# Two buffers for the softmax sums, hops of the sums and of x set later than their producers, and w_in split at its first use

## The chip, the cores and the metric

The kernel runs on one core of one Trainium2 chip. The metric is the device time of one execution in microseconds; each time is a median of several runs of the same program. The core has five engines with queues of their own: TensorE (PE in the profile, its weight loads PEld), VectorE (DVE), ScalarE (ACT), GpSimd (POOL) and SyncE (SP), which here issues the DMAs of all loads and stores but the gathers and scatters of the last stage. Each queue is worked off in its order; an instruction at the head that waits holds what stands behind it.

## The reference

```python
q_n, k_n = rmsnorm(q, g_q), rmsnorm(k, g_k)              # 4 batches, 12 heads, 448 rows, 64 columns
attn = softmax(q_n @ k_n.T / sqrt(64))                   # sums + 1e-9 as the divisor
x = (attn @ v) with the heads side by side               # 1792 x 768
h = x @ w_in                                             # 768 x 2048, w_in in 64-bit floats
x = (h * clip(h + 3, 0, 6) / 6) @ w_out                  # 2048 x 768, w_out in 64-bit floats
logits = x @ w_gate                                      # 8 experts, each takes 224 rows, greedily
out[rows of e] = relu(x[rows of e] @ w1[e]) @ w2[e]
```

## The kernel before

All products run on float32 data split in a high and a low part (`xh`, `xl`; `wh`, `wl`), three matmuls for each product of two split operands. The attention is done in 24 head pairs, six to a batch. The first MLP product of a batch (16 units of 128 columns of `w_in`, 18 matmuls each) is cut in atoms and laid between the attention of the next batch's pairs; the last batch's follows the attention, and then come the second product, the routing and the experts, which the change does not touch.

The order of the attention stage is written by hand. `at(t, fn, ...)` enters an event at place t of a list; pair i begins at t = 16 i, and the constants `T_...` (L70 to L81) are places relative to that. The list is sorted, and every engine's queue gets its instructions in that order; `fill` hands out MLP atoms evenly in between, so that batch b's units lie between the places `ENDS[b]` and `ENDS[b+1]` (117 and 217 for batch 0, 313 for batch 1, 405 for batch 2). An event may stand ahead of another one's last use of the same buffer: it then waits.

For the pairs 6 to 22 the sums of the softmax make a way through memory: `padd` (GpSimd, L423) adds the exponentials `ph`, `psums` (L435) sums them on TensorE with a matrix of ones and copies the result with ScalarE into `rb` (L441, place 15.7), `rs_out` stores it (L445), `rs_in` loads it back in another layout (L450), `rec` takes reciprocals on DVE (L454), `r_out` stores them (L458), `r_in` loads them, broadcast, into the same `rb` (L464), `xmul` multiplies on GpSimd (L468), and `xsplit` makes `xh` on ScalarE (L478) and `xl` on GpSimd (L476). `rb` has one buffer. The pairs 0 to 5 and 23 take another way (L384 to L415) with no hops.

`w_in` and `w_out` arrive as 64-bit floats. `conv` (L148) narrows a unit: a load `wraw`, a copy on ScalarE (L139) and three operations on DVE (L140 to L142) into `cv` (two buffers), and a store to `w32` or `wo32` (L181, L179). For `w_in` it also makes the split: the high part on ScalarE (L171), the low part on GpSimd (L174), both in `whl` (one buffer), stored as `w_hl` (L176). The units of `w_in` lie at the places 20 + 10 u, those of `w_out` at 180 + 12 u. The first MLP products of the batches 0 to 2 then load a unit whole from `w_hl` (`win_whole`, L196, at atom `WD2` of the unit two before). For batch 3 `win_load` reads `w32` into a staging buffer and `win_split` (L191) makes both parts: high on ScalarE (L116), low on DVE for odd units and on GpSimd for even ones (L117). The tile `w` has three buffers. `g_out` stores a unit's result at atom `GD` of the next one.

Of the kernel before, what the change touches and what calls it, by code (L numbers as in the profile page):

```python
# [8 lines left out]
F32 = mybir.dt.float32  # L9
F32R = mybir.dt.float32r  # L10
BF16 = mybir.dt.bfloat16
I32 = mybir.dt.int32
AF = mybir.ActivationFunctionType
OP = mybir.AluOpType
# [7 lines left out]
def kernel(  # L22
# [14 lines left out]
    nc = tc.nc  # L37
    B, H, S, D = q.shape
# [5 lines left out]
    CP = 112  # L44
    NCH = S // CP
    NP = H // 2
    NC = DM // 128
    NF = FF // 128
    NTC = NT // 128
    NSL = NT // CP  # L50
    VB, CB = 4, 2
    WB = 6
    OB = 3
    PB = 12
# [12 lines left out]
    GR_, GG = 3, 2  # L67
    CI, CI0, CI1, CI2, CO = 6, 1.75, 2.5, 0.5, 1.5

    T_LOAD, T_VLOAD, T_NORM, T_Q, T_K, T_V = -72, -8, -38, -30, -28, 6  # L70
    T_SUMS, T_INV = -50, -42
    T_S1, T_MT = (-24, -23.9, -16, -15.9), -9
    T_ST = (0, 0.1, 8, 8.1)
    T_AV = ((17, 18, 19.5, 20.5), (22, 23, 24.5, 25.5))
    T_NUM, T_XT, T_MLP = 28, 33, (37, 41, 41, 37)
    T_ADD, T_PV, T_SUM = (6, 13), (15.6, 15.62, 15.64, 15.66), 15.7
    T_RS, T_RL, T_REC, T_RO, T_RB, T_X, T_XH, T_XL = 18, 21, 24, 25.5, 29, 35, 36, 38
    GD, WD2 = 6, 8
    C_ST, C_WH, C_WL, C_HL = 6, 7, 10, 13
    QMAJOR = tuple(range(NP)) + (B * NP - 1,)  # L80
    T_CI, D_CI, T_CO, D_CO, T_CL = 20, 10, 180, 12, 14  # L81

# [6 lines left out]
    dram = ctx.enter_context(tc.tile_pool(name="dram", bufs=1, space=DRAM))  # L89
# [34 lines left out]
    rawp = raw_stack.enter_context(tc.tile_pool(name="rawp", bufs=1, side="right"))  # L124
# [7 lines left out]
    wide = w_in.dtype == mybir.dt.int64  # L132
# [9 lines left out]
                lambda: nc.vector.scalar_tensor_tensor(vi, hi, -2147483648, vi, op0=OP.bitwise_and, op1=OP.bitwise_or))  # L142

    RAW = {}
    wide_b = range(B - 1) if wide else ()
    w_hl = [dram.tile([128, 2, 768], F32, name=f"w_hl{u}") for u in range(NF if wide else 0)]

    def conv(key, part):  # L148

        out_, n = key  # L150
        rows = slice(n * 128, (n + 1) * 128)
        if part < 0:
            raw = rawp.tile([128, 768, 2], I32, name="wraw", bufs=2)
            if out_:
                nc.sync.dma_start(raw.rearrange("p f t -> p (f t)"), w_out.bitcast(I32)[rows, :])
            else:
                nc.sync.dma_start(raw.rearrange("p (c f) t -> p c (f t)", c=NC),
                                  w_in.bitcast(I32)[:, n * 256:(n + 1) * 256].rearrange("(c p) f -> p c f", p=128))
            RAW[key] = raw
            return  # L160
        if part == 0:
            raw = RAW[key]
            v32 = rawp.tile([128, 768], F32, name="cv", bufs=CB)
            RAW[key] = (v32, narrow(raw[:, :, 0], raw[:, :, 1], v32))
        v32, steps = RAW[key][:2]
        if part < 4:
            steps[part]()
        elif part == C_WH:
            hl = rawp.tile([128, 2, 768], F32R, name="whl", bufs=1)
            RAW[key] += (hl,)  # L170
            nc.scalar.activation(hl[:, 0], v32, AF.Copy)  # L171
        elif part == C_WL:
            hl = RAW[key][2]
            nc.gpsimd.tensor_tensor(hl[:, 1], v32, hl[:, 0].bitcast(F32), op=OP.subtract)  # L174
        elif part == C_HL:
            nc.sync.dma_start(w_hl[n], RAW[key][2].bitcast(F32))  # L176
        elif part == C_ST:
            if out_:
                nc.sync.dma_start(wo32[rows, :], v32)  # L179
            else:  # L180
                nc.sync.dma_start(w32[:, rows].rearrange("(c p) f -> p c f", p=128), v32.rearrange("p (c f) -> p c f", c=NC))  # L181
# [4 lines left out]
    def win_load(u):  # L186
        v32 = stage("win_v").rearrange("p (c f) -> p c f", c=NC)
        nc.sync.dma_start(v32, src_in[:, u * 128:(u + 1) * 128].rearrange("(c p) f -> p c f", p=128))
        return u, v32

    def win_split(u, v32):  # L191
        w = wpool.tile([128, 2, NC, 128], F32R, name="w", bufs=WB // 2)
        split(v32, w[:, 0], w[:, 1], nc.vector if u % 2 else nc.gpsimd)
        return w[:, 0], w[:, 1]

    def win_whole(u):  # L196
        w = wpool.tile([128, 2, NC, 128], F32R, name="w", bufs=WB // 2)
        nc.sync.dma_start(w.rearrange("p a c f -> p a (c f)").bitcast(F32), w_hl[u])
        return w[:, 0], w[:, 1]


    a_stack = ExitStack()
    apool = a_stack.enter_context(tc.tile_pool(name="apool", bufs=2, side="left"))
# [32 lines left out]

    def vload(i):
        b, j = divmod(i, NP)
        t = apool.tile([CP, 2, NCH, D], F32, name="ld_v", bufs=1)
        nc.sync.dma_start(t.rearrange("p h c d -> p h (c d)"),  # L240
                          v[b, 2 * j:2 * j + 2].rearrange("h (p c) d -> p h (c d)", p=CP))
        QKV[i].append(t)
# [175 lines left out]
    PA, PV, RC, RB = {}, {}, {}, {}  # L418
# [16 lines left out]
    def psums(i):  # L435
        p = ps.tile([128, 512], F32, name="sm", tag="b", bufs=8)
        for n in range(2):
            for s, r in enumerate(ROWS):
                nc.tensor.matmul(p[r, :S], ones64, PA.pop((i, s, n)), start=(n == 0), stop=(n == 1))
        RB[i] = apool.tile([128, S], F32, name="rb", bufs=1)  # L440
        nc.scalar.activation(RB[i], p[:, :S], AF.Identity, bias=eps)  # L441

    def rs_out(i):
# [37 lines left out]

    late, tpool, ready, loaded = [], [], [], []
    units_in = list(range(NF)) * B
    whole = [len(wide_b) * NF]
    GB = 2

    def prefetch(splits=2):

        while whole[0] and len(ready) < splits:
            ready.append(win_whole(units_in.pop(0)))  # L490
            whole[0] -= 1
        if whole[0]:
            return
        while len(ready) < splits and loaded:
            ready.append(win_split(*loaded.pop(0)))
        while units_in and len(loaded) < 3 and (len(units_in) > NF or len(loaded) + len(ready) < 3 or tpool):
            loaded.append(win_load(units_in.pop(0)))

    def mlp1_atoms(b, inline):

        atoms = []
        state = {}

        def unit_start(f):
            if not ready:
                prefetch(1)
            if not ready:
                prefetch(1)
            state["w"] = ready.pop(0)
            if not whole[0]:  # L510
                prefetch()
            state["ps"] = ps.tile([128, 512], F32, name="h", tag="b", bufs=8)

        def mm(f, n):
            if n == 0:
                unit_start(f)
            c, t = divmod(n, 3)
            wh, wl = state["w"]
            xh, xl = XT[b]
            w = (wh, wh, wl)[t]  # L520
            x = (xh, xl, xh)[t]
            p = state["ps"]
            nc.tensor.matmul(p[:, :S], w[:, c], x[:, c], start=(n == 0), stop=(n == 3 * NC - 1))  # L523
            if n == 3 * NC - 1:
                r = mpool.tile([128, S], F32, name="r", bufs=1)
                nc.scalar.activation(r, p[:, :S], AF.Relu, bias=half, scale=1.0 / 6.0)
                g = mpool.tile([128, S], F32, name="g", bufs=GB)
                nc.vector.scalar_tensor_tensor(g, r, 1.0, p[:, :S], op0=OP.min, op1=OP.mult)
                state["g", f] = g
                if inline:  # L530
                    gsplit(b, f, g, nc.vector)

        def g_out(f):
            nc.sync.dma_start(g_dr[b][f * 128:(f + 1) * 128, :], state.pop(("g", f)))

        for f in range(NF):
            for n in range(3 * NC):
                atoms.append(lambda f=f, n=n: mm(f, n))
                if n == GD and f > 0:
                    atoms.append(lambda f=f: g_out(f - 1))  # L540
                if n == WD2 and b in wide_b:
                    atoms.append(prefetch)
                if inline and n == 10 and f > 1:
                    atoms.append(lambda f=f: lg(b, f - 2))
        atoms.append(lambda: g_out(NF - 1))
        if inline:
            for f in (NF - 2, NF - 1):
                late.append(lambda f=f: lg(b, f))
            late.append(lambda: lg_end(b, 0))
            late.append(lambda: lg_end(b, 1))  # L550
        return atoms
# [183 lines left out]
    for i in range(NH // 2):  # L735
        t = 16 * i
# [35 lines left out]
    for u in range(NF if wide else 0):  # L772
        for out_, t in ((0, T_CI + D_CI * u), (1, T_CO + D_CO * u)):
            at(t - T_CL, conv, (out_, u), -1)
            for part in (0, 1, 2, 3, C_ST) + (() if out_ else (C_WH, C_WL, C_HL)):
                at(t + part, conv, (out_, u), part)
    events.sort(key=lambda e: e[:2])
    ENDS = [8 * H * (b + 1) - 16 + T_MLP[b] for b in range(B)]
# [1 line left out]
    for t, _, fn, args in events:  # L780
        while now <= t:
            b = min(sum(now > e for e in ENDS), B - 1)
            end = ENDS[b]
            left = end - now
            w = 1
            if b == B - 1:
                z = end - max(now, 8 * NH + 4)
                left += (WT - 1) * z
                w = WT if now >= 8 * NH + 4 else 1
# [260 lines left out]
    for t in range(NTC):  # L1050
        a, z = t * 128, t * 128 + 128
# [130 lines left out]
    for pi, (t, hfs) in enumerate(passes):  # L1182
# [10 lines left out]
        for f in range(NF):  # L1193
            i, k = divmod(f, QF)
# [7 lines left out]
            wh, wl = wo[f]  # L1202
# [131 lines left out]
```

## Time and profile before

| | us |
|---|---|
| median of 3 runs | 1263.83 (1259.71 to 1263.83) |
| profiled execution, its own time | 1260.03 |
| its span, first to last instruction | 1258.2 |
| TensorE busy | 1161.1 (92%) |
| DVE busy | 779.1 (62%) |
| ScalarE busy | 549.4 (44%) |
| GpSimd busy | 505.8 (40%) |
| mean granted TensorE clock | 0.964 of full speed |

One execution was profiled. A matmul's end is modelled, so a busy TensorE need not be at its peak. Up to about 138 us of the span batch 0's attention runs alone, from there to about 565 us attention and MLP units are interleaved, to about 690 us the last batch's MLP runs, and then the rest. The granted clock has two levels, 1.2 and 2.4 GHz; a stretch's number is the mean of 0.5 and 1.

### The profile page before, as it was taken

Reading aid. Unit: us, or ns where it says so; the run is one execution under the profiler, and the core shown is the slowest. Engines: PE = TensorE matmul, PEld = TensorE weight load, DVE = VectorE, ACT = ScalarE, POOL = GpSimd, SP = SyncE. Lnnn points to the kernel's source line nnn. Section 1 sums busy time; section 2 is a strip of 40 time slices with the busy share of each in tenths; the row PEclk is TensorE's granted clock in tenths of the full one; section 3 lists DMA queues with packets and bytes.
Section 4 is the critical chain, followed back from the end, with each engine's and each line's share of the span. In section 5 each row is a group of like instructions: output and inputs, shape, how many; then the busy total and the mean of one; then the engine's idle time right before and its main releaser. Section 6 shows DMA issues by size and latency. Waiting matters only on the chain.

```text
span 1258.2 us, 19791 instructions
## 1 busy us (share of the span) xinstructions
PE 1161.1 (92%) x7204; PEld 943.5 (75%) x7204; DVE 779.1 (62%) x1572; ACT 549.4 (44%) x1019; POOL 505.8 (40%) x370
## 2 busy tenths in 40 slices
PE   4979998888999889999988999999999799999997
PEld 2777665665666667687766777777777799999997
DVE  7977866566567566424886466666667574555550
ACT  3645644543444445444664311111112575556650
POOL 2323654453344343211344222222224477766641
PEclk9977999899999999999998999999999899999999
DMA  3556898756655776656987422222224788877731
GB/s 106 176 192 205 277 317 258 265 195 209 239 208 193 242 238 242 237 181 197 304 261 236 129 76 61 71 63 76 64 76 118 213 249 257 244 236 236 223 123 44
DMA packets 200469, 237.14 MB, mean 188 GB/s; under 512 B 24338, under 2 KB 171444, under 8 KB 200372
## 3 DMA queue, kind: packets, MB, share of 16 engines
q1 hardware_dynamic: 197044, 224.88, 56.8%
q0 software_dynamic: 3328, 11.01, 2.8%
q8 instruction: 56, 0.92, 0.3%
q14 instruction: 41, 0.34, 0.1%
HBM read 184.87 MB, written 50.98 MB: 187 GB/s over the span
## 4 chain that ended last, share of the span: by engine, by line
PE 45%; DVE 7%; issue 5%; DMA 4%; ACT 2%; POOL 1%; POOLq 0%; SPq 0%; DVEq 0%; ACTq 0%
PE y L1138 15%; PE y L1286 8%; PE h L523 6%; PE h L1222 5%; PE h L1224 2%; DMA wo_s<-wo 2%; DMA we_s<-in_moe_w_dram 2%; PE rt L948 2%; DVE C L943 1%; DVE gl L561 1%; PE st L341 1%; PE av L430 1%; PE h L662 1%; PE xp L1170 1%; DVE wel L117 1%
## 5 line engine op out<-in xcount | busy, mean ns | idle before, releaser
L523 PE MATMUL h<-xh,w 128*128 128x448 f32 x768 | 245.2, 389 | 4.2 <-DVE mr L330 4.1
L523 PEld LDWEIGHTS h<-xh,w 128*128 128x128 f32 x768 | 147.4, 197 | 35.3 <-issue 16.1
L1081 POOL TENSOR_TENSOR g2l<-gr,g2h 128x512 fp32r<-128x512 f32 x60 | 79.1, 1320 | 206.7 <-ACT g2h L1079 159.5
L322 DVE TENSOR_REDUCE mx<-s 112x1 f32<-112x448 f32 x192 | 106.9, 613 | 70.0 <-PE s L319 69.9
L523 PE MATMUL h<-xl,w 128*128 128x448 f32 x384 | 147.0, 383 | 0.0
L1138 PE MATMUL y<-woh,g2l 128*128 128x512 f32 (+1 forms) x448 | 128.8, 349 | 1.0 <-POOL g2l L1081 1.0
L1079 ACT ACTIVATE g2h<-gr 128x512 fp32r<-128x512 f32 x60 | 37.9, 631 | 206.2 <-PE y L1138 158.5
L1138 PE MATMUL y<-woh,g2h 128*128 128x512 f32 (+1 forms) x448 | 127.7, 348 | 0.0
L1138 PE MATMUL y<-wol,g2h 128*128 128x512 f32 (+1 forms) x448 | 126.4, 346 | 0.0
L117 DVE TENSOR_TENSOR wel<-we_s,weh 128x768 fp32r<-128x768 f32 x59 | 78.7, 1341 | 60.6 <-ACT weh L116 60.6
L117 POOL TENSOR_TENSOR wel<-we_s,weh 128x768 fp32r<-128x768 f32 x48 | 97.1, 2028 | 44.5 <-ACT weh L116 37.9
L116 ACT ACTIVATE weh<-we_s 128x768 fp32r<-128x768 f32 x107 | 88.3, 841 | 60.1 <-DMA we_s<-in_moe_w_dram 41.8
L352 ACT ACTIVATE ph<-st 112x448 f32<-112x448 f32 x192 | 92.2, 545 | 41.5 <-PE st L341 41.1
L1222 PE MATMUL h<-xe,weh 128*128 128x448 f32 x318 | 100.3, 375 | 2.2 <-DVE xe L1173 2.2
L423 POOL TENSOR_TENSOR pa<-ph 112x448 f32<-112x448 f32 x68 | 88.4, 1320 | 7.5 <-ACT ph L352 7.5
L523 PEld LDWEIGHTS h<-xl,w 128*128 128x128 f32 x384 | 75.1, 196 | 10.1 <-issue 3.6
L1138 PEld LDWEIGHTS y<-woh,g2l 128*128 128x128 f32 x448 | 73.1, 190 | 10.8 <-POOL g2l L1081 1.3
L1138 PEld LDWEIGHTS y<-woh,g2h 128*128 128x128 f32 x448 | 72.8, 190 | 10.6 <-issue 1.2
L1138 PEld LDWEIGHTS y<-wol,g2h 128*128 128x128 f32 x448 | 72.5, 190 | 9.7
L1224 PE MATMUL h<-xe,wel 128*128 128x224 f32 x318 | 76.6, 268 | 0.0
L1286 PE MATMUL y<-weh,hl 128*112 128x384 f32 x216 | 73.0, 338 | 0.0
L1286 PE MATMUL y<-weh,hh 128*112 128x384 f32 x216 | 72.9, 337 | 0.0
(258 smaller groups left out, 2527.3 us busy)
## 6 DMA issues: line engine op xcount, KB each, us to landing
we_s<-in_moe_w_dram SPq DMA_DIRECT2D x128, 384.0 KB, 4.4
w<-w_hl SPq DMA_DIRECT2D x48, 768.0 KB, 5.9
g_dr<-g SPq DMA_DIRECT2D x64, 224.0 KB, 2.9
gr<-g_dr SPq DMA_DIRECT2D x52, 256.0 KB, 2.9
wraw<-in_moe_w_in_dram SPq DMA_DIRECT2D x16, 768.0 KB
w_hl<-whl SPq DMA_DIRECT2D x16, 768.0 KB, 5.2
wraw<-in_moe_w_out_dram SPq DMA_DIRECT2D x16, 768.0 KB, 6.4
gr<-g_dr SPq DMA_DIRECT2D x48, 224.0 KB, 3.5
```

The lines of the kernel that those rows point to most:

```text
L116: nc.scalar.activation(hi, raw, AF.Copy)
L117: eng.tensor_tensor(lo, raw, hi.bitcast(F32), op=OP.subtract)
L322: mx = nc.vector.tensor_reduce(MX[i][:, s, c:c + 1], pp[s][:CP, :S], axis=AX.X, op=OP.max)
L352: nc.scalar.activation(e, pp[s][:CP, :S], AF.Exp)
L423: nc.gpsimd.tensor_tensor(PA[i, s, n], PP[i, s, 2 * n][0], PP[i, s, 2 * n + 1][0], op=OP.add)
L523: nc.tensor.matmul(p[:, :S], w[:, c], x[:, c], start=(n == 0), stop=(n == 3 * NC - 1))
L1079: nc.scalar.activation(gh, g, AF.Copy)
L1081: eng.tensor_tensor(gl, g, gh.bitcast(F32), op=OP.subtract)
L1138: nc.tensor.matmul(pp[hf][:, :COLS[hf].stop - COLS[hf].start], a[:, f % QF], w[:, COLS[hf]], start=(f == 0 and n == 0), stop=(f == NF - 1 ...
L1222: mm = [lambda: nc.tensor.matmul(p[:, :4 * CP], wh[:, fo], x.rearrange("d k t -> d (k t)"), start=(c == 0), stop=(c == NC - 1), skip_group ...
L1224: lambda: nc.tensor.matmul(p[:, :2 * CP], wl[:, fo], x[:, 0], start=False, stop=False, skip_group_check=True)]
L1286: nc.tensor.matmul(p[:CP, :HW], a[:, f, tk], w[:, o], start=(f == 0 and n == 0), stop=(f == FB - 1 and n == 2))
```

## The change

`rb` gets two buffers, and so does `ld_v`, whose load comes four places earlier. The hops get new places: `rs_out` 18 to 19.5, `rs_in` 21 to 21.5, `r_in` 29 to 28, `xmul` 35 to 33, `xh` 36 to 35.5, `xl` 38 to 39.5. The conversion of `w_in` makes no split any more and stores only `w32`, a place earlier, and `cv` has one buffer. Batch 0's units are loaded from `w32` and split there, like batch 3's; each unit's `w` tile is then stored as `w_hl` when the unit begins, and the batches 1 and 2 load it whole. In these two batches loads are issued at atom 8 alone. `g` is stored at atom 12 in place of 6.

```diff
-    VB, CB = 4, 2
+    VB, CB = 4, 1
-    T_LOAD, T_VLOAD, T_NORM, T_Q, T_K, T_V = -72, -8, -38, -30, -28, 6
+    T_LOAD, T_VLOAD, T_NORM, T_Q, T_K, T_V = -72, -12, -38, -30, -28, 6
-    T_RS, T_RL, T_REC, T_RO, T_RB, T_X, T_XH, T_XL = 18, 21, 24, 25.5, 29, 35, 36, 38
-    GD, WD2 = 6, 8
-    C_ST, C_WH, C_WL, C_HL = 6, 7, 10, 13
+    T_RS, T_RL, T_REC, T_RO, T_RB, T_X, T_XH, T_XL = 19.5, 21.5, 24, 25.5, 28, 33, 35.5, 39.5
+    GD, WD2, C_ST = 12, 8, 5
-    wide_b = range(B - 1) if wide else ()
+    whole_b = range(1, B - 1)
...
-        elif part == C_WH:
-            hl = rawp.tile([128, 2, 768], F32R, name="whl", bufs=1)
-            RAW[key] += (hl,)
-            nc.scalar.activation(hl[:, 0], v32, AF.Copy)
-        elif part == C_WL:
-            hl = RAW[key][2]
-            nc.gpsimd.tensor_tensor(hl[:, 1], v32, hl[:, 0].bitcast(F32), op=OP.subtract)
-        elif part == C_HL:
-            nc.sync.dma_start(w_hl[n], RAW[key][2].bitcast(F32))
...
-        t = apool.tile([CP, 2, NCH, D], F32, name="ld_v", bufs=1)
+        t = apool.tile([CP, 2, NCH, D], F32, name="ld_v", bufs=2)
...
-        RB[i] = apool.tile([128, S], F32, name="rb", bufs=1)
+        RB[i] = apool.tile([128, S], F32, name="rb", bufs=2)
...
-    whole = [len(wide_b) * NF]
+    fetched = [0]
     def prefetch(splits=2):
-        while whole[0] and len(ready) < splits:
-            ready.append(win_whole(units_in.pop(0)))
-            whole[0] -= 1
-        if whole[0]:
-            return
+        def whole():
+            return units_in and fetched[0] // NF in whole_b and not loaded
+        def take():
+            fetched[0] += 1
+            return units_in.pop(0)
         while len(ready) < splits and loaded:
             ready.append(win_split(*loaded.pop(0)))
-        while units_in and len(loaded) < 3 and (len(units_in) > NF or len(loaded) + len(ready) < 3 or tpool):
-            loaded.append(win_load(units_in.pop(0)))
+        while len(ready) < splits and whole():
+            ready.append(win_whole(take()))
+        while (units_in and fetched[0] // NF not in whole_b and len(loaded) < 3
+               and (len(units_in) > NF or len(loaded) + len(ready) < 3 or tpool)):
+            loaded.append(win_load(take()))
...
-            if not whole[0]:
+            if b == 0:
+                nc.sync.dma_start(w_hl[f], state["w"][2].rearrange("p a c f -> p a (c f)").bitcast(F32))
+            if b not in whole_b:
                 prefetch()
...
-                if n == WD2 and b in wide_b:
+                if n == WD2 and b in whole_b:
...
-            for part in (0, 1, 2, 3, C_ST) + (() if out_ else (C_WH, C_WL, C_HL)):
+            for part in (0, 1, 2, 3, C_ST):
```

## Rows read from the trace of the kernel before

**Rows 1.** The page's busy us, share of the span and instructions.
```profile
PE 1161.1 (92%) x7204; PEld 943.5 (75%) x7204; DVE 779.1 (62%) x1572; ACT 549.4 (44%) x1019; POOL 505.8 (40%) x370
```

**Rows 2.** Waits of TensorE, 138 to 565 us: us in total, times, longest us.
```profile
PE s L319 <- ACT rb L441: 12.1, 5, 4.2
PE st L341 <- ACT rb L441: 5.1, 2, 3.7
PE h L523 <- DVE mr L330: 4.1, 2, 2.0
PE s L319 <- DVE g L528: 3.0, 2, 2.3
PE t L296 <- ACT rb L441: 2.5, 1, 2.5
```

**Rows 3.** The same view for ScalarE and GpSimd, 138 to 565 us.
```profile
ACT rb L441 <- POOL xn_t L468: 41.9, 10, 7.0
...
POOL xn_t L468 <- DMA rb<-rec_dr: 93.8, 16, 12.1
```

**Rows 4.** Timeline, one turn: start us, us, instruction, idle before it and releaser.
```profile
236.29 1.67 PE L439 MATMUL sm<-pa,ones 112*64 112x448 f32 x8
...
242.01 1.13 POOL L468 TENSOR_TENSOR xn_t<-xn_t,rb 128x448 f32<-128x448 f32 x1 [6.33 <-DMA rb<-rec_dr]
243.16 0.63 ACT L441 ACTIVATE rb<-sm,eps 128x448 f32<-128x448 f32 x1 [6.02 <-POOL xn_t L468]
...
243.85 0.71 PE L341 MATMUL st<-qh,kh 64*112 64x448 f32 x1 [3.67 <-ACT rb L441]
```

**Rows 5.** Timeline of batch 0's attention, around the conversion of two units.
```profile
57.42 0.37 SPq L181 DMA_DIRECT2D w<-cv  x1
...
61.12 0.91 ACT L139 ACTIVATE cv<-wraw 128x768 f32<-128x768 f32 x1
...
61.84 0.40 SPq L176 DMA_DIRECT2D w_hl<-whl  x1
...
68.03 0.84 ACT L171 ACTIVATE whl<-cv 128x768 fp32r<-128x768 f32 x1 [3.27 <-DMA w_hl<-whl]
...
69.45 0.98 PE L413 MATMUL t<-ident,num 112*128 112x112 f32 x4 [4.19 <-ACT ph L352]
```

**Rows 6.** Stretches: us, busy PE, PEld, DVE, ACT, POOL, clock, DMA share, GB/s.
```profile
69.40:85.80 16.40, 16.35 (x87) 15.08 (x87) 10.12 (x25) 7.79 (x16) 3.41 (x3) 0.50 0.51 169
138.00:252.00 114.00, 103.77 (x553) 70.86 (x553) 74.42 (x125) 56.64 (x104) 60.02 (x43) 0.93 0.84 280
252.00:565.00 313.00, 290.40 (x1691) 206.61 (x1691) 180.96 (x336) 145.05 (x293) 115.34 (x95) 0.98 0.65 218
```

**Rows 7.** Instructions on `rb`: ns min/median/max, first and last start us, forms.
```profile
L441 ACT ACTIVATE rb<-sm,eps x17: 633/634/636, 144.7 to 536.5; 128x448 f32<-128x448 f32 x17
```

**Rows 8.** The same view: batch 3's splits, and a conversion step up to 260 us.
```profile
L117 POOL TENSOR_TENSOR w<-win_v,w x8: 1840/1854/2246, 573.0 to 654.6; 128x768 fp32r<-128x768 f32 x8
L117 DVE TENSOR_TENSOR w<-win_v,w x8: 947/955/959, 579.5 to 661.3; 128x768 fp32r<-128x768 f32 x8
...
L141 DVE SCALAR_TENSOR_TENSOR cv<-wraw,cv x17: 942/951/1784, 44.3 to 257.6; 128x768 int32<-128x768 int32 x17
```

**Rows 9.** DMA issues: count, KB each, median us from issue to landing.
```profile
w<-w_hl SPq DMA_DIRECT2D x48, 768.0 KB, 5.9
...
w_hl<-whl SPq DMA_DIRECT2D x16, 768.0 KB, 5.2
...
w<-cv SPq DMA_DIRECT2D x16, 384.0 KB, 3.2
...
win_v<-w SPq DMA_DIRECT2D x16, 384.0 KB, 5.6
```

**Rows 10.** Waits of SP's queue, 138 to 565 us, as in rows 2.
```profile
SPq L445 <- ACT ph L352: 38.9, 10, 5.8
SPq L464 <- DMA rec_dr<-rs: 29.4, 13, 6.1
```

More of the change, by code (lines that the diff above doesn't have):

```diff
@@ L144 @@
     RAW = {}
-    wide_b = range(B - 1) if wide else ()
-    w_hl = [dram.tile([128, 2, 768], F32, name=f"w_hl{u}") for u in range(NF if wide else 0)]
+    whole_b = range(1, B - 1)
+    w_hl = [dram.tile([128, 2, 768], F32, name=f"w_hl{u}") for u in range(NF)]
     def conv(key, part):
@@ L164, in conv @@
             RAW[key] = (v32, narrow(raw[:, :, 0], raw[:, :, 1], v32))
-        v32, steps = RAW[key][:2]
+        v32, steps = RAW[key]
         if part < 4:
             steps[part]()
-        elif part == C_WH:
-            hl = rawp.tile([128, 2, 768], F32R, name="whl", bufs=1)
-            RAW[key] += (hl,)
-            nc.scalar.activation(hl[:, 0], v32, AF.Copy)
-        elif part == C_WL:
-            hl = RAW[key][2]
-            nc.gpsimd.tensor_tensor(hl[:, 1], v32, hl[:, 0].bitcast(F32), op=OP.subtract)
-        elif part == C_HL:
-            nc.sync.dma_start(w_hl[n], RAW[key][2].bitcast(F32))
         elif part == C_ST:
@@ L193, in win_split @@
         split(v32, w[:, 0], w[:, 1], nc.vector if u % 2 else nc.gpsimd)
-        return w[:, 0], w[:, 1]
+        return w[:, 0], w[:, 1], w
     def win_whole(u):
@@ L198, in win_whole @@
         nc.sync.dma_start(w.rearrange("p a c f -> p a (c f)").bitcast(F32), w_hl[u])
-        return w[:, 0], w[:, 1]
+        return w[:, 0], w[:, 1], w
     a_stack = ExitStack()
@@ L517, in mm @@
             c, t = divmod(n, 3)
-            wh, wl = state["w"]
+            wh, wl, w = state["w"]
             xh, xl = XT[b]
-            w = (wh, wh, wl)[t]
+            lhs = (wh, wh, wl)[t]
             x = (xh, xl, xh)[t]
             p = state["ps"]
-            nc.tensor.matmul(p[:, :S], w[:, c], x[:, c], start=(n == 0), stop=(n == 3 * NC - 1))
+            nc.tensor.matmul(p[:, :S], lhs[:, c], x[:, c], start=(n == 0), stop=(n == 3 * NC - 1))
             if n == 3 * NC - 1:
```

## The prediction

> **What bounds the kernel now.** I read the page's busy rows first, then the stretches of the attention stage, then who TensorE waited for in it, then who ScalarE waited for, and last single turns in the timeline. TensorE is busy 92% of the span [rows 1], so only its holes can be had: time in which it has nothing, and time at the lower clock level. Between 138 and 565 us three kinds of work are interleaved on it (scores, sums, and units of the first MLP product), and its longest waits there have one source: 12.1 us before L319, 5.1 before L341 and 2.5 before L296, all behind the ScalarE instruction that writes `rb`, L441 [rows 2]. Together that is 19.7 us. The next sources are two of DVE, with 4.1 and 3.0.
>
> ScalarE in turn stood 41.9 us, ten times and up to 7.0 us, before L441 until GpSimd's L468 had finished [rows 3]. L468 is the last reader of the **previous** head pair's `rb`, and there is one buffer. GpSimd itself stood 93.8 us before L468 for the DMA that brings the reciprocals back into `rb` [rows 3]. One turn shows it: the sums' matmuls start at 236.29 and last 1.67, L468 starts only at 242.01, L441 at 243.16 after 6.02 us of waiting, and TensorE's next L341 at 243.85 after 3.67 us [rows 4]. The sums were ready at 237.96; ScalarE stood with the exponentials, the MLP's relu and all else queued behind it.
>
> A second place lies in batch 0's attention. The store of `whl` is issued at 61.84, ScalarE needs that single buffer again for L171 and gets it at 68.03 after 3.27 us, and TensorE's L413 starts at 69.45 after a 4.19 us wait [rows 5]. From 69.4 to 85.8 TensorE is then busy all the time, at a granted clock of 0.50, the level of 1.2 GHz [rows 6].
>
> **The change, part by part.** All terms are against the profiled execution, 1260.0 us (span 1258.2 and 1.8 around it); the median of the runs is 0.3% above it.
>
> (1) *Second `rb`.* L441 of pair i+1 then waits for L468 of pair i-1, a whole turn earlier: that wait goes. What is late next is the step behind it on ScalarE that still needs L468 of pair i, the copy `xh` (L478). The 17 turns run from 144.7 to 536.5 [rows 7]: 391.8 us for 16 turns of 16 places of the event list is 1.53 us a place. L478 now lies at 16i+35.5 and L441 of the next pair at 16i+31.7, so L478 comes 3.8 places or 5.8 us later. The longest wait today is 7.0 us [rows 3], so at most 1.2 us of it can stand again there, in one or two turns. I take -19.7 + 1.2 = **-18.5**. Bounds: -19.7, and 0 if the hops slip so far that all of it comes back (below).
>
> (2) *Clock behind those waits.* 114 us at 0.93 and 313 us at 0.98 [rows 6] are 114 x 0.07 + 313 x 0.02 = 14.3 us of lost TensorE time, at most. The holes behind `rb` are 19.7 of the 26.8 us of the five longest waits [rows 2], nearly three quarters, but the clock need not follow each. I take **-8**; bounds 0 and -14.3.
>
> (3) *`whl` goes.* Sixteen L171 (ScalarE), 16 L174 (GpSimd) and 16 stores leave the conversion. The one stall that is seen to reach TensorE there cost it 4.19 us [rows 5]. Of the 16.4 us at half clock, TensorE's work would take 8.2 at full clock, but DVE has 10.12 us of its own in it [rows 6], so no more than 6.3 is to be had, and only if the clock does stay up. I take -4.2 and half of 6.3: **-7**; bounds 0 and -10.5.
>
> (4) *The split moves into batch 0's MLP.* It costs what `whl`'s copy of the same shape (0.84 us on ScalarE [rows 5]) and the subtractions of batch 3's units show, 1.854 us on GpSimd or 0.955 on DVE by turns [rows 8]. Sixteen are 13.4 us of ScalarE, 14.8 of GpSimd, 7.6 of DVE in batch 0's 100 places or 153 us, where ScalarE, DVE and GpSimd had 57, 40 and 54 us free in the first 114 [rows 6]; the conversions that run in that stretch lose their L171 and L174. The work is made two units ahead, so TensorE meets it only when an engine's queue is held. A DVE instruction with two inputs from on-chip memory took between 0.942 and 1.784 us (L141) [rows 8], so eight DVE splits may cost 6.6 us more. I take **+3**, bounds 0 and +10.
>
> On that the Trainium skill has a rule against the change: GPSIMD Engine Reference, section 1 (Specifications), says that GpSimd shares its interfaces to SBUF with VectorE and contends with DVE instructions that have two SBUF inputs. The spread of L141 agrees; were every DVE split held so on the path, the sum would be 1239.
>
> (5) *DMAs of batch 0.* A unit is now read as 384 KB from `w32` (5.6 us to landing, against 5.9 for the 768 KB of `w_hl`) and its 768 KB stored from `w` (5.2) [rows 9]. It is loaded five units ahead, so its latency is covered; a unit takes 153 / 16 = 9.6 us. The store holds the tile of unit f until it has landed, and the split of unit f+3 on ScalarE needs that tile: covered as long as SP issues the store less than 9.6 - 5.2 = 4.4 us late. 0 in the sum; without the cover, the slower rival below. The DMA engines were 0.84 busy from 138 to 252 [rows 6], and bytes hardly change: 16 x (384 + 768) KB now, and 16 x 768 KB with the stores of those conversions that fell there before.
>
> The Trainium skill (DMA: Bandwidth & Descriptors, Specifications) names 512 B as enough for line rate; half the bytes, in pieces of that size, should then take clearly less. The landing times, 5.6 against 5.9, do not show that; by the rule the queue of the hops would empty a little and the first rival below lose half its chance.
>
> (6) *One `cv` buffer.* L139 of the next unit must now wait for the store of this one. In the turn shown the store is issued at 57.42 and the next L139 is at 61.12 [rows 5], 3.7 us for a landing of 3.2 [rows 9]: 0.5 us to spare. Some of the ten units before 138 us will stand up to 1 us. **+2**; bounds 0 and +8 (a stall as long as L171's 3.27, twice, and its holes).
>
> (7) *Hops and the other queues.* The first hop moves 1.5 places later on SP, and `rs` in 0.5; SP stood at the first hop ten times, 38.9 us in all, waiting for ScalarE's exponentials, that is, before the sums were made [rows 10]. So SP arrives early and the move only lets loads past. The last hop moves a place earlier, where SP already stood 29.4 us in 13 turns for the reciprocals' store [rows 10]: no earlier landing. The product L468 comes two places earlier on GpSimd, which waits there anyway; what is queued behind it (norms, sums, splits) has GpSimd's idle half for cover. `g` is stored six matmuls later and the next load goes first: 0. The second `ld_v` with the load four places earlier: 0. I take **0**; bounds -2 and +5.
>
> (8) *Batch 2 to 3.* The first loads for batch 3 wait for the middle of the last units, as the call at each unit's start is gone in batch 2. **+1**; bounds 0 and +4.
>
> Sum: -18.5 - 8 - 7 + 3 + 0 + 2 + 0 + 1 = -27.5, so 1232.5 for the profiled execution. The median stands 0.3% higher, of which I carry half: **1234**.
>
> **Rivals.** (A) *The wait moves to `xh`.* If the landing of `rb` slips by what the first hop moved, 1.5 places or 2.3 us, the longest waits (ten with a mean of 4.2, against a cover of 5.8 - 2.3 = 3.5) come back at L478 for some ten us of ScalarE, of which TensorE feels 19.7 / 41.9, some 5, and half the clock's 8 is lost: 1234 + 4 + 4 = 1242. For it: GpSimd always waits for that DMA. Against: SP's early arrival. Chance 0.18. (B) *Batch 0's attention does not gain.* DVE, 10.12 us of 16.4 even at the lower level [rows 6], and the single `cv` set the pace and the clock falls anyway: terms (3) and (6) become 0 and +6, 1234 + 7 + 4 = 1245. Chance 0.13. (C) *No measurable change:* A in full, with no gain in (1) and (2): 1234 + 26.5 = 1260.5. Chance 0.11. (D) *Slower: ScalarE stands for the store of `w_hl`.* SP also carries the hops, and stands there for 2.3 us in the mean and 6.1 at most [rows 10]. From 4.4 us of lateness on, each unit of batch 0 stops ScalarE; a whole unit late it is 5.2 us x 16 = 83 us, of which TensorE feels 0.47, 39 us, plus the clock's 8: 1234 + 47 = 1281. Against it: the places where SP waits are spread, and it arrives early at most. Chance 0.10.
>
> **How the numbers follow.** Forecast 0.48, A 0.18, B 0.13, C 0.11, D 0.10. All gains with no cost would be 1260 - 19.7 - 14.3 - 10.5 = 1215.5; I set the low end at 1218, as not all come together. At the high end, A and B together are 1253, which leaves 5 us for their own bounds: 1258. Left out are C and D, 0.21, and a little of the forecast's low end. Within 0.5%, about what a measurement can tell from no change, is 1257.5 to 1270.2. Faster: forecast, A, B: 0.79, less some for their tails: 0.76. Same: C and those tails, 0.14. Slower: D, 0.10.
>
> **What would show it.** L441 with no wait for L468, and L478 with a total under 5 us (1); fewer half-clock stretches between 138 and 565 (2); no wait of 3 us before a conversion step, and the clock at 0.9 or more between 65 and 90 us (3); ScalarE's splits with no wait for a DMA of `w_hl` (5, D); L139 waits for the store under 1 us each (6). The forecast is wrong if the place where TensorE waited for `rb` shows another wait of like length, on `xh`, a split or GpSimd's sums.

## The result, and the profile after

| | before | after |
|---|---|---|
| median, us | 1262.89 (1259.71 to 1263.83, 4 runs) | 1214.95 (1213.70 to 1219.53, 4 runs) |
| profiled execution | 1260.03 | 1219.53 |
| mean granted TensorE clock | 0.964 | 0.978 |

The ratio is 0.9631 [0.96, 0.9662]. The sign was right and the size was not: 47.9 us went where 29 were forecast, and the time lies 3 us below the range. Some of that is scatter: the profiled execution of after is the longest of its four, 4.6 us above their median, and that of before is 2.9 below its own. Between the two profiled executions, which are all that the two traces can explain, 40.5 us went, against a sum of 27.5.

The line numbers move by about ten: L441 is now L431, L468 (product) L458, L478 (`xh`) L468, L476 (`xl`) L466, the high part of a split L115, its low part L116, the conversion's copy L138. The page's busy rows, to set beside [rows 1]:

```profile
PE 1145.3 (94%) x7204; PEld 931.2 (76%) x7204; DVE 780.7 (64%) x1580; ACT 552.1 (45%) x1019; POOL 490.6 (40%) x362
```

The work is the same, but for eight subtractions that go from GpSimd to DVE; the holes are fewer. To see where they closed I cut both traces at the same points of the work: where DVE writes a pair's row of maxima (`mr`). Stretches of the kernel before, pairs 3 to 5 and 7 to 22 (columns as in [rows 6]):

```profile
58.60:101.50 42.90, 35.75 (x232) 31.85 (x228) 29.45 (x56) 22.18 (x42) 15.71 (x12) 0.70 0.65 202
135.80:497.10 361.30, 328.16 (x1822) 227.44 (x1820) 229.58 (x403) 169.18 (x319) 162.15 (x126) 0.96 0.71 238
```

And the same pairs in the kernel after:

```profile
60.50:92.20 31.70, 27.90 (x236) 24.30 (x234) 26.02 (x54) 17.71 (x36) 6.25 (x6) 0.89 0.61 170
126.20:456.40 330.20, 319.70 (x1839) 222.06 (x1835) 234.06 (x411) 177.93 (x328) 162.73 (x125) 0.99 0.80 260
```

Pair 7 is reached at 126.4 (the window begins 0.2 us ahead of it) in place of 135.8: 9.5 us from batch 0's attention (pair 3 still comes 2.1 later than before), where terms (3) and (6) gave 5. The interleaved stage, pairs 7 to 22, takes 330.2 in place of 361.3: 31.1 us, where terms (1), (2) and (4) gave 23.5. Of these 31.1, 22.6 are idle time of TensorE (361.30 - 328.16 = 33.1 before, 10.5 after) and 8.5 are busy time, at a mean granted clock of 0.99 in place of 0.96. Behind pair 22 nothing changes by more than 1 us. So both stages gained more than forecast. The waits of TensorE over the interleaved pairs in the kernel after, 126.2 to 456.4 us (us in total, times, longest us; compare [rows 2]), show no `rb` any more:

```profile
PE s L309 <- ACT ph L342: 2.1, 2, 1.7
PE st L331 <- DVE kl L298: 1.7, 2, 1.1
PE s L309 <- DVE g L525: 1.5, 2, 1.1
```

ScalarE's in the same stretch: `rb` now waits only for the sums themselves, and no longer for the product.

```profile
ACT rb L431 <- PE sm L429: 15.0, 11, 3.0
...
POOL xl L466 <- ACT xh L468: 9.3, 10, 2.0
```

(The second line is GpSimd's, from the same view and stretch; it is needed below.)

### The profile page after: what moved, and what is told of

The parts are those of the page before. It is cut to its first block, busy times and chain, and to the rows that moved or that the text cites. A ratio compares the mean times of both kernels' runs of the same rounds, so it can differ in the third digit from the quotient of the medians.

```text
span 1217.7 us, 19761 instructions
## 1 busy us (share of the span) xinstructions
PE 1145.3 (94%) x7204; PEld 931.2 (76%) x7204; DVE 780.7 (64%) x1580; ACT 552.1 (45%) x1019; POOL 490.6 (40%) x362
## 4 chain that ended last, share of the span: by engine, by line
PE 62%; DVE 14%; DMA 9%; issue 6%; ACT 4%; POOL 2%; SPq 1%; POOLq 0%; DVEq 0%; ACTq 0%
PE y L1135 16%; PE h L520 10%; PE y L1283 8%; PE h L1219 5%; PE st L331 4%; PE av L420 3%; PE av L371 3%; PE h L1221 2%; PE sm L429 2%; PE rt L945 2%; DMA gr<-g_dr 1%; DMA wo_s<-wo 1%; PE s L309 1%; DVE C L940 1%; DMA we_s<-in_moe_w_dram 1%
## 5 line engine op out<-in xcount | busy, mean ns | idle before, releaser
L520 PE MATMUL h<-xh,w 128*128 128x448 f32 x768 | 240.3, 381 | 0.6 <-DVE mr L320 0.3
L520 PEld LDWEIGHTS h<-xh,w 128*128 128x128 f32 x768 | 144.8, 192 | 30.6 <-issue 14.3
L1135 PE MATMUL y<-wol,g2h 128*128 128x512 f32 (+1 forms) x448 | 126.4, 346 | 0.0
L116 DVE TENSOR_TENSOR wel<-we_s,weh 128x768 fp32r<-128x768 f32 x59 | 80.6, 1372 | 61.5 <-ACT weh L115 59.2
L115 ACT ACTIVATE weh<-we_s 128x768 fp32r<-128x768 f32 x107 | 88.9, 842 | 59.3 <-DMA we_s<-in_moe_w_dram 41.1
L116 POOL TENSOR_TENSOR wel<-we_s,weh 128x768 fp32r<-128x768 f32 x48 | 95.5, 1991 | 46.7 <-ACT weh L115 36.0
L413 POOL TENSOR_TENSOR pa<-ph 112x448 f32<-112x448 f32 x68 | 85.8, 1282 | 53.6 <-ACT ph L342 53.4
```

Source lines behind the costliest of these rows:

```text
L115: nc.scalar.activation(hi, raw, AF.Copy)
L116: eng.tensor_tensor(lo, raw, hi.bitcast(F32), op=OP.subtract)
L413: nc.gpsimd.tensor_tensor(PA[i, s, n], PP[i, s, 2 * n][0], PP[i, s, 2 * n + 1][0], op=OP.add)
L520: nc.tensor.matmul(p[:, :S], lhs[:, c], x[:, c], start=(n == 0), stop=(n == 3 * NC - 1))
L1135: nc.tensor.matmul(pp[hf][:, :COLS[hf].stop - COLS[hf].start], a[:, f % QF], w[:, COLS[hf]], start=(f == 0 and n == 0), stop=(f == NF - 1 ...
```

## Experiments

The theory at the outset was the prediction's: the second `rb` carries the gain, the hops' places carry none. The rivals were that the places matter by themselves, that the moved split does, and that the conversion's relief does. Runs that stand together share a chip, and the time of the kernel before that is given with them is from that chip; the kernel after has runs of its own of the kernel before (1262.89), so a few us between it and another group say little, and the ratios are given with the times.

**The ladder: the change put on in three steps.** With one `rb` buffer the moved split can't keep GpSimd: ScalarE's next `rb` would wait for GpSimd's product, that product would stand behind a split's low part, and that behind the high part, which stands behind the same `rb` on ScalarE, a circle. So, as argued from the order of the queues (no run has that form), the second buffer is a condition for that part of the change, and the run with one buffer takes batch 0's low parts to DVE. A run with two buffers and the same DVE splits stands beside it.

```diff
 # hops_only: the kernel before, with the new places
-    T_RS, ... = 18, 21, 24, 25.5, 29, 35, 36, 38
+    T_RS, ... = 19.5, 21.5, 24, 25.5, 28, 33, 35.5, 39.5
 # after_dve: the kernel after; after_dve_rb1 has the second edit too
-        split(v32, w[:, 0], w[:, 1], nc.vector if u % 2 else nc.gpsimd)
+        split(v32, w[:, 0], w[:, 1], nc.vector if u % 2 or len(units_in) >= 2 * NF else nc.gpsimd)
-        RB[i] = apool.tile([128, S], F32, name="rb", bufs=2)
+        RB[i] = apool.tile([128, S], F32, name="rb", bufs=1)
```

> The kernel before with the new places of the hops alone, one buffer of rb, conversion with whl. Theory: rb's writer still waits for the product, which still waits for the DMA of the reciprocals: 1258 to 1266, no change that can be measured. Rival (the places are the cause): under 1245.

> The same, with the one buffer of rb put back, and nothing else. Theory (the wait of rb's writer for the product of the pair before is what the change took away): TensorE's waits behind rb come back with about 20 us and the lower clock with about 9, so 1215 + 29 = 1244. Rival (the new places of the hops, with the product two places earlier, already take the wait away, and the second buffer adds little): no more than 1225.

> The changed kernel, with all sixteen splits of batch 0 on DVE (L116 in its place on DVE, none on GpSimd). It is the base for the next run. If the time of a split is hidden, as the result suggests, 1215 us within 4 either way. If the splits cost what the prediction's term (4) had (+3, and up to 6.6 more for held DVE instructions), then twice as many on DVE give 1219 to 1225.

The kernel before took 1259.43 on the chip of these runs; hops_only 1251.59, ratio 0.9949 [0.9921, 0.9978]; after_dve_rb1 1240.19, 0.985 [0.9812, 0.9889]; after_dve 1216.00, 0.9651 [0.961, 0.9691]. The steps are 7.8 us for the places alone, 11.4 for split, conversion and loads, 24.2 for the second buffer; giving half of the splits back to GpSimd changes nothing that can be told (0.9631 against 0.9651, with overlapping intervals). Cut at the same pairs, the profiled executions of before, hops_only, after_dve_rb1 and after_dve reach pair 7 at 135.8, 136.6, 128.0 and 125.2 us and take 361.3, 356.4, 353.9 and 331.1 from there to pair 22. So split, conversion and loads gain ahead of pair 7, the buffer behind it, and the places some 5 us there; another 3.4 of theirs lie behind pair 22, where they move nothing. In after_dve_rb1 the wait of [rows 3] is there at full size. TensorE's and ScalarE's first wait, 126 to 500 us:

```profile
PE s L309 <- ACT rb L431: 17.0, 9, 4.4
...
ACT rb L431 <- POOL xn_t L458: 46.4, 11, 7.1
```

So all that is gained without the buffer is gained elsewhere: these 17.0 us are hardly less than the 19.7 of [rows 2]. The places gain 8 us with the `rb` wait still there (TensorE 18.2 us behind L441 in hops_only, over the same stretch), which term (7) did not allow for.

**The places undone in the kernel after.**

```diff
 # after_oldhops
-    T_RS, ... = 19.5, 21.5, 24, 25.5, 28, 33, 35.5, 39.5
+    T_RS, ... = 18, 21, 24, 25.5, 29, 35, 36, 38
```

> The changed kernel with the hops at their old places (18, 21, 24, 25.5, 29, 35, 36, 38) and two buffers of rb. Theory: the places are worth little, since the writer of rb no longer waits: 1215 to 1220. Rival A of the prediction turned round (without the new places ScalarE's copy xh takes the wait over): 1230 or more.

1227.33 (1225.2 to 1229.1), ratio 0.9747 [0.9707, 0.9788]: 11.3 us more than after_dve on the same chip, and 12.4 more than the kernel after. Pairs 12 to 18 carry 9.0 of it; after_oldhops first, then the kernel after (columns as in [rows 6]):

```profile
240.30:379.30 139.00, 131.02 (x729) 92.16 (x728) 95.16 (x161) 67.09 (x122) 62.44 (x50) 0.96 0.71 232
```

```profile
239.60:369.60 130.00, 125.78 (x721) 88.06 (x720) 87.92 (x161) 66.93 (x122) 61.03 (x50) 0.99 0.75 254
```

GpSimd's waits in after_oldhops, 126 to 500 us, show what changed: it stands 71.0 us for `xh`, where the kernel after shows 9.6 over the same stretch.

```profile
POOL xl L466 <- ACT xh L468: 71.0, 14, 9.9
```

**Which place it is.** One place each was set back: `xl` alone, the product and `xh`, the hops on SP.

```diff
 # after_xl38: T_XL 39.5 -> 38
 # after_x35:  T_X 33 -> 35, T_XH 35.5 -> 36
 # after_rs18: T_RS, T_RL 19.5, 21.5 -> 18, 21; T_RB 28 -> 29
```

> The changed kernel with one hop moved back: xl on GpSimd at place 38 in place of 39.5, so that it stands ahead of the next pairs' sums in GpSimd's queue again. Of the 12 us that all old places cost, theory xl (GpSimd stood 71.0 us before xl with the old places against 9.6 with the new, and what is behind it came late) says that most is here: 1222 to 1228. Theory product (the product two places earlier is what counts) and theory store (the first hop's place on SP) both say 1213 to 1218 here.

> The changed kernel with the product back at 35 and xh back at 36, xl staying at 39.5. Theory product: 1222 to 1228. Theories xl and store: 1213 to 1218.

> The changed kernel with SP's hops back (18, 21 and 29), the rest new. Theory store: 1222 to 1228. Theories xl and product: 1213 to 1218.

Against 1264.73 before: 1221.97, ratio 0.9652 [0.9591, 0.9713]; 1219.44, 0.9636 [0.9576, 0.9695]; 1214.83, 0.9594 [0.9532, 0.9655]. The intervals of the three overlap, but every run of after_xl38 (1218.5 to 1227.7) and of after_x35 (1217.2 to 1222.6) took longer than every run of after_rs18 (1210.6 to 1216.7). So the old places of the hops on SP cost nothing that shows, and both other places seem to cost something, 7.1 and 4.6 us by the medians; the times do not rank these two. The profiled executions (here, as of the kernel after, the longest of the four) point to `xl`: pairs 12 to 18 take 132.2 us in after_x35, but in after_xl38

```profile
238.80:377.10 138.30, 129.31 (x727) 90.76 (x726) 92.53 (x161) 66.81 (x122) 62.33 (x50) 0.98 0.72 242
```

138.3, which is 8.3 of the 9.0. Pairs 7 to 22 take 342.4 us in after_xl38, 334.3 in after_x35 and 330.2 in the kernel after; what the product's and `xh`'s places cost by stays open. For `xl`, one turn shows how. Timeline of the kernel after, GpSimd and DVE:

```profile
272.07 1.15 POOL L458 TENSOR_TENSOR xn_t<-xn_t,rb 128x448 f32<-128x448 f32 x1 [10.83 <-DMA rb<-rec_dr]
273.18 2.26 POOL L413 TENSOR_TENSOR pa<-ph 112x448 f32<-112x448 f32 x2
276.73 1.17 POOL L466 TENSOR_TENSOR xl<-xn_t,xh 128x448 fp32r<-128x448 f32 x1 [1.28 <-ACT xh L468]
...
278.01 0.18 DVE L254 TENSOR_SCALAR st<-st 112x32 int32<-112x32 int32 x1
278.23 0.19 DVE L256 SCALAR_TENSOR_TENSOR st<-st 112x32 f32<-112x32 f32 x1
...
280.38 1.05 POOL L269 TENSOR_TENSOR xn<-ld_q,st 112x512 f32<-112x512 f32 x1 [2.49 <-PE st L331]
```

The same turn of after_xl38, and TensorE's next wait:

```profile
272.14 1.15 POOL L458 TENSOR_TENSOR xn_t<-xn_t,rb 128x448 f32<-128x448 f32 x1 [11.47 <-DMA rb<-rec_dr]
...
276.84 1.16 POOL L466 TENSOR_TENSOR xl<-xn_t,xh 128x448 fp32r<-128x448 f32 x1 [3.55 <-ACT xh L468]
...
277.95 2.26 POOL L413 TENSOR_TENSOR pa<-ph 112x448 f32<-112x448 f32 x2
278.12 1.02 DVE L254 TENSOR_SCALAR st<-st 112x32 int32<-112x32 int32 x1
279.17 1.09 DVE L256 SCALAR_TENSOR_TENSOR st<-st 112x32 f32<-112x32 f32 x1
...
282.66 0.47 PE L520 MATMUL h<-xh,w 128*128 128x448 f32 x1 [1.76 <-DVE mr L320]
```

At place 39.5, `xl` stands behind two additions (L413) of the pair two on (its place 6 is place 38 of `xl`'s pair), and GpSimd makes these while ScalarE makes `xh`. At 38 it stands ahead of them: GpSimd waits 3.55 us, and the additions then run beside DVE's small block for the norms (L253 to L258). Two DVE instructions of 0.18 and 0.19 us take 1.02 and 1.09, the block comes late, and with it the maxima behind it on DVE, for which TensorE stands 1.76 us. That chain is read from one turn, but its signs are in the kernel before too, and go with the places alone. Three lines of before, 126 to 500 us (the last is L264, which is L254 of the kernel after), and the same three of hops_only:

```profile
POOL xl L476 <- ACT xh L478: 76.4, 12, 9.8
...
PE h L523 <- DVE mr L330: 4.1, 2, 2.0
...
L264 DVE TENSOR_SCALAR st<-st 112x32 int32<-112x32 int32 x7 | 5.4, 771 | 0.5
```

```profile
POOL xl L476 <- ACT xh L478: 13.7, 11, 2.9
...
PE h L523 <- DVE mr L330: 0.6, 2, 0.3
...
L264 DVE TENSOR_SCALAR st<-st 112x32 int32<-112x32 int32 x7 | 1.3, 181 | 0.5
```

To test the chain, `xl` was left at 38 and DVE's block for the norms set 1.5 places later. That takes it from just ahead of a pair's maxima to just behind them (counted from that pair, the block moves from -10 to -8.5 and the maxima stand at -9). A second run of after_xl38 stood beside it.

```diff
 # xl38_inv: after_xl38, and the norms' block later
-    T_SUMS, T_INV = -50, -42
+    T_SUMS, T_INV = -50, -40.5
```

> As the run with xl back at 38, but DVE's block that inverts the norms' sums 1.5 places later (-40.5 in place of -42), as far from GpSimd's sums as in the changed kernel. Theory collision (xl ahead of the sums makes GpSimd's sums late, so that they run while DVE inverts; DVE's instructions are held, as L254 with 911 ns against 309, and the row of maxima behind them holds TensorE): L254 back near 309 ns and the time at 1213 to 1218. Theory order (the late sums themselves hold TensorE): still 1220 to 1226.

> The run with xl back at 38, again on this chip: 1219 to 1226 by either theory.

Against 1260.97 before: xl38_inv 1218.73 (1211.3 to 1227.2), ratio 0.9662 [0.9619, 0.9704]; xl38_again 1223.37 (1221.0 to 1229.8), 0.9702 [0.9669, 0.9734]. Pairs 12 to 18 take 132.6 us in xl38_inv, 137.2 in xl38_again and 130.0 in the kernel after; pairs 7 to 22 take 334.2, 341.4 and 330.2. L254 by shape, 126 to 465 us (busy us, mean ns), in the kernel after, in xl38_again and in xl38_inv:

```profile
L254 DVE TENSOR_SCALAR st<-st 112x32 int32<-112x32 int32 x7 | 2.2, 309 | 0.5
```

```profile
L254 DVE TENSOR_SCALAR st<-st 112x32 int32<-112x32 int32 x7 | 5.5, 780 | 0.5
```

```profile
L254 DVE TENSOR_SCALAR st<-st 112x32 int32<-112x32 int32 x7 | 3.8, 548 | 0.5
```

The held instructions do not all go away: L254 is at 548 ns, not back at 309. The same turn in xl38_inv shows what did change:

```profile
280.27 2.26 POOL L413 TENSOR_TENSOR pa<-ph 112x448 f32<-112x448 f32 x2
280.31 0.62 DVE L320 TENSOR_TENSOR mr<-t,place 128x448 fp32r<-128x448 f32 x1
...
281.49 1.08 DVE L254 TENSOR_SCALAR st<-st 112x32 int32<-112x32 int32 x1
```

The block still meets the additions, but the maxima now stand ahead of it, and between 276 and 291 us TensorE shows no wait for them. Most of the stretch comes back, as the chain from the late block over the maxima to TensorE would have it. That GpSimd's additions are what holds the block is read from the turns alone. The intervals of the two times overlap, and no run sets the block later in the kernel after, where the new order might gain too: so this points to the chain and does not settle it.

**The second buffer alone.** In the kernel before there is no memory for it, so one of the twelve `ph` buffers was given up, in a control too.

```diff
 # pb11, and in rb2_pb11 and rb2_hops_pb11 too
-    PB = 12
+    PB = 11
 # rb2_pb11 and rb2_hops_pb11
-        RB[i] = apool.tile([128, S], F32, name="rb", bufs=1)
+        RB[i] = apool.tile([128, S], F32, name="rb", bufs=2)
 # rb2_hops_pb11: the new T_RS, ... as in hops_only
```

> The kernel before with 11 buffers of the exponentials ph in place of 12: the base for the next two, which need the space. 1258 to 1268 if the twelfth buffer is not needed; more if it is.

> The same with two buffers of rb and nothing else of the change: what the prediction's terms (1) and (2) were about. By them 26 us faster than the base; by the run that put one buffer back, 24. Rival (with the old places GpSimd stands for xh and takes back a part, as in the run with the old places): 10 to 18 us faster.

> The same with the new places of the hops as well, conversion and split as before. If the places and the buffer add up as they did singly (8 to 12, and 24): 32 to 36 us faster than the base. If the places only pay with the buffer, or the reverse: near 24.

Against 1264.84 before: pb11 1279.71, ratio 1.0132 [1.0079, 1.0185]; rb2_pb11 1248.64, 0.9871 [0.9821, 0.9921]; rb2_hops_pb11 1253.21, 0.9899 [0.985, 0.9949]. The buffer alone is worth 31.1 us. The interleaved stage, pairs 7 to 22, in pb11 and then in rb2_pb11 (columns as in [rows 6]):

```profile
152.40:517.10 364.70, 330.23 (x1820) 228.93 (x1820) 230.26 (x404) 168.68 (x317) 163.00 (x127) 0.95 0.71 235
```

```profile
152.50:487.80 335.30, 321.06 (x1820) 223.97 (x1820) 231.07 (x403) 170.52 (x317) 163.51 (x127) 0.97 0.78 256
```

It shrinks by 29.4: TensorE's idle time by 20.2, from 34.5 to 14.2, and its busy time for the same 1820 matmuls by 9.2, with the granted clock up from 0.95 to 0.97. Terms (1) and (2) had 18.5 and 8. (As an undo, after_dve_rb1 to after_dve, the two are 13.8 and 9.0.) TensorE's waits, 138 to 565 us, of pb11:

```profile
PE s L319 <- ACT rb L441: 11.6, 5, 4.7
PE st L341 <- ACT rb L441: 6.7, 2, 5.0
PE h L523 <- DVE mr L330: 4.1, 2, 2.1
```

and of rb2_pb11, where `mr` stands first and no `rb` is left:

```profile
PE h L523 <- DVE mr L330: 3.9, 2, 2.0
```

The new places on top bring nothing here (+4.6, the intervals overlap). The trace says part of why: over the pairs 13 to 21 they gain 10.5 us (182.4 to 171.9), but from pair 10 to 13 they lose 18 (59.4 to 77.5), and there ScalarE stands for the one `whl` buffer, 11.7 us in two times, a step that the kernel after no longer has. The rest of the 18 stays open. One of the two:

```profile
265.25 0.84 ACT L171 ACTIVATE whl<-cv 128x768 fp32r<-128x768 f32 x1 [7.87 <-DMA w_hl<-whl]
```

**The conversion's part.** In the kernel before, `whl` was cut in two tiles and the high half stored five places earlier, so that the wait of [rows 5] goes and the work stays.

```diff
 # whl_halves: the kernel before
-            hl = rawp.tile([128, 2, 768], F32R, name="whl", bufs=1)
+            hl = [rawp.tile([128, 768], F32R, name=f"whl{k}", bufs=1) for k in range(2)]
 # high half stored at place 8, low half at 13 as before
```

> The kernel before with whl as two tiles of half the size, each stored by itself: the high part right after ScalarE made it (place 8), the low part as before. Same work, same bytes, same space; ScalarE's next copy waits only for the first half's store. Theory wait (what held batch 0's attention up was ScalarE standing for the 768 KB store): the pairs 3 to 5 take 32 to 36 us from pair 3's to pair 5's row of maxima, against 42.9 before and 31.7 in the changed kernel, and the whole is 6 to 11 us faster than before. Rival work (the copies, subtractions and stores themselves): still 41 to 44 us there, no change that can be measured.

Against 1263.74 before: 1262.91 (1260.6 to 1267.9), ratio 0.9998 [0.9974, 1.0022]: no gain. The wait is gone, though, and pairs 3 to 5 take 37.3 us, about half way from 42.9 to 31.7:

```profile
59.10:96.40 37.30, 32.21 (x229) 28.67 (x228) 29.19 (x55) 22.10 (x42) 15.70 (x12) 0.78 0.80 241
```

Pair 7 comes 4.3 us earlier; by pair 10 that is lost, and by pair 20 the kernel is 4.6 behind. ScalarE's waits for the product are 41.1 us there, no more than the 41.9 of [rows 3], so these do not account for the loss. Between the pairs 8 and 10, where it falls, TensorE stands 2.9 us for a load of `w` from `w_hl`, a wait that the kernel before does not show there; the loss at pair 20 stays open. The other attempt, the old work put back into the kernel after (the split done as before and stored where nothing reads it), can't be read:

```diff
 # put_back_store: the kernel after, and in the conversion (in words)
+        7: whl[:, 0] = copy of cv (ScalarE);  10: whl[:, 1] = cv - whl[:, 0] (GpSimd);  13: store whl
 # whl and ld_v with one buffer
```

> The changed kernel with the old conversion's split put back beside it, unused: per unit of w_in the copy on ScalarE and the subtraction on GpSimd into one buffer whl, and its 768 KB store to a place that nobody reads (ld_v gives up its second buffer for the space). Theory wait (ScalarE standing for that store held TensorE 4 us in batch 0's attention and let the clock fall): TensorE's wait of 3 to 4 us is back, 1215 + 8 to 12 = 1223 to 1227. Rival (the gain before 138 us came from the less work or from elsewhere, not from this wait): under 1220.

Against 1264.73 before: 1261.43, ratio 0.9962 [0.9933, 0.9991], far more than the work's price. In this kernel the subtraction holds the single `cv`, and ScalarE's next conversion waits for it (24.4 us in 12 times, 40 to 280 us), and for the added store (25.7 in 7), and SP stands 61.7 us for the one `ld_v`. It prices none of the three by itself.

**The smaller terms.** One buffer for `ld_v` with the early load kept; batch 0's units fetched at atom 8 as those of the batches 1 and 2; two `cv`; the last two together.

```diff
 # after_v1: ld_v bufs=2 -> 1
 # after_split8: "if b not in whole_b: prefetch()" -> "if b == B - 1", "if n == WD2 and b in whole_b" -> "b < B - 1"
 # after_cv2: CB = 1 -> 2
 # split8_cv2: both
```

> The changed kernel with one buffer of ld_v, its load staying at the earlier place. It tells what the run with the split put back was slow by. Theory ld_v (SP stands at that load until ScalarE has read the pair before's v, and every other transfer behind it comes late; SP's wait there was 61.7 us between 40 and 280 us in that run): 1225 to 1255, with such waits of SP. Rival (the work put back, with one cv buffer held for it, did it): 1212 to 1218.

> The changed kernel with batch 0's splits issued at atom 8 of a unit in place of its start, as the loads of the batches 1 and 2 are: the store of the tile to be reused gets eight matmuls more to land. If ScalarE's 10.3 us of waits for that store (rival D of the prediction, in small) reach TensorE: 1207 to 1212. If they are hidden: 1213 to 1218.

> The changed kernel with two buffers of cv. By the prediction's term (6) the one buffer costs 2 us: 1211 to 1214. If ScalarE's waits for the store of w32 (2.9 us from 126 us on, 4.0 before) are hidden: 1213 to 1218.

> The changed kernel with batch 0's splits at atom 8 and two buffers of cv, each of which was 4 us faster alone. If their waits are separate ones: 1206 to 1209. If both remove the same wait: 1210 to 1212.

Against 1263.74 before (split8_cv2: 1264.84): after_v1 took 1222.52, ratio 0.9674 [0.9641, 0.9708]; after_split8 1210.76, 0.9606 [0.9566, 0.9646]; after_cv2 1211.04, 0.9583 [0.9551, 0.9615]; split8_cv2 1211.47, 0.9572 [0.9534, 0.9611]. The second `ld_v` looks worth some 7 us (its interval overlaps that of the kernel after a little); the three others lie 4 us below the kernel after with intervals that overlap its own, and together they bring no more than each alone. None is clearly better than the kernel after.

## Why the prediction was off, point by point

- **(7), hops' places: the step that failed.** It was put at 0 with bounds -2 and +5; undone in the kernel after, the places cost 11 to 12 us, and alone in the kernel before they gain 8. I asked of each moved step whether it would come earlier, and answered from SP's waits [rows 10] and from the landing that GpSimd waits for. Of SP that was right (after_rs18 is no slower than the kernel after). I did not ask what stands *behind* `xl` on GpSimd: the additions for a later pair, which could be made while ScalarE makes `xh`. I gave "GpSimd's idle half" as cover, but that half was made of such waits in a fixed order. The longest of them does not stand in [rows 3], whose line for GpSimd is the second; over the same 138 to 565 us of the kernel before it is

```profile
POOL xl L476 <- ACT xh L478: 101.3, 15, 9.8
```

  and the 4.1 us behind `mr` in [rows 2], which I passed over, were its trace on TensorE: they go to 0.6 with the places alone. With -12 in place of 0 the forecast is 1222; and without the places the change took 1227.33, 7 us below the forecast and inside the range. The low end, 1218, stood on the best cases of (1) to (3), 1215.5, in which the places had no part; the result, 1214.95, lies below even that. (In term (2), 114 x 0.07 + 313 x 0.02 is 14.2, not 14.3, which moves nothing.)
- **(1) and (2), buffer and clock: right.** Forecast 26.5; measured 24.2 as an undo and 31.1 alone, with idle and busy time near the two terms. Rival A did not come: ScalarE shows no wait of `xh` for the product in the kernel after. Rival C fell with it.
- **(3) and (6), batch 0's attention: the mechanism right, the size short.** Forecast 5, found 9.5. The wait for `whl` went, and the stretch 69.4 to 85.8 us has a granted clock of 0.79 in place of 0.50 [rows 6]. That is short of the 0.9 that I named as a sign (0.86 from 65 to 90 us). whl_halves shows that the wait alone gives about half of the gain of pairs 3 to 5; that the rest is the work and bytes taken out is argued from what remains, not shown. There the gain was lost again further on, but not because of the `rb` waits: after_dve_rb1 has them at full size and keeps to the end the 8.6 us that it has over hops_only at pair 7. Rival B did not come.
- **(4), moved split: +3 forecast, no cost seen.** No run prices it by itself: split, conversion and loads together make pairs 7 to 22 shorter by 2.5 us (hops_only to after_dve_rb1). The eight DVE splits were held, as feared: L116 took 946 to 3445 ns, 11.5 us for eight, 3.8 more than at 0.955 each, where I had allowed 6.6. But none of TensorE's waits is for a split.
- **(5) and rival D: the wait exists and is small.** I wrote that a split with a wait for the store of `w_hl` would prove the step wrong. There are four, 10.3 us in all:

```profile
ACT w L115 <- DMA w_hl<-w: 10.3, 4, 4.3
```

  So the cover fails at times, but no more than four times in sixteen; after_split8 still shows 9.7 us of it. It does not reach TensorE as a wait for a split.
- **(6), single waits: wrong in length.** I wrote under 1 us each; 126 to 565 us has two, up to 2.5:

```profile
ACT cv L138 <- DMA w<-cv: 2.9, 2, 2.5
```

  The price, +2, is of the right order: after_cv2 lies 4 below, not clear of its interval.
- **`ld_v`, put at 0 within (7):** some 7 us by after_v1, not clear of the intervals. With one buffer the early load only moves SP's wait: SP stands 76.1 us in 14 times for the values' last reader, with loads and hops queued behind it.
- **(8):** not found. From pair 22 to the end, where it falls, the profiled executions take 761.1 us before and 761.3 after.

The terms also do not add. The places gain 8 in the kernel before, 12 in the kernel after and nothing in rb2_hops_pb11; whl_halves gains 4 us and gives them back, while the whole change to the conversion keeps its gain. A sum of terms, each taken at today's bound, does not hold such dependences.

## What to carry to other kernels

For each moved instruction ask two things of its queue: when can it run, and what could have run while it waits. An engine that is idle half the time can still be late, because in a fixed order its idle time stands in front of instructions that were ready. And where a change removes several waits in a row, do not trust the sum of the pieces: undo each part in the kernel after as well as trying it alone in the kernel before, since here the answers for one part were 12, 8 and 0 us.

## What the runs showed of the hardware

- A small DVE instruction can be held many times its length beside GpSimd's additions: L254 took 0.18 us with GpSimd idle (277.90 to 280.38 in the kernel after) and 1.02 us beside an addition in after_xl38. The Trainium skill (GPSIMD Engine Reference, Specifications) names contention with DVE instructions that have two SBUF inputs or a two-port mode. The turn above agrees in so far as the held L256 (0.19 to 1.09 us) has two inputs; the held L254 reads a single tile, and which port mode it ran in no row shows.
- Holes of 2 us on TensorE, which look harmless beside a stretch of 139 us, come with a lower clock: the mean granted clock of pairs 12 to 18 was 0.96 in after_oldhops and 0.99 in the kernel after. As an estimate, 139.0 x 0.04 less 130.0 x 0.01, that is 4.3 of the 9.0 us; TensorE's busy time there differs by 5.2.
- Eleven in place of twelve `ph` buffers cost 15 us, all of it in batch 0's attention (pair 7 at 152.4 against 135.8), with ScalarE standing 39.1 us for them; nothing in the trace of before showed that the twelfth was in use.
